# The second weight's sums on VectorE and later in the down stage; weight pieces one a step early in that stage

## The chip, the cores and the metric

One core of one Trainium2 chip. The metric is device microseconds of one launch. The six runs of the kernel before lie within 0.3% of one another (1125.70 to 1128.74 us), its eleven in the session of e17 and e18 within 0.7% (1124.67 to 1131.90 us), so an effect of 0.5% needs several runs of both kernels, interleaved. All runs told here were in the fast state and all gave correct results.

## The reference, cut to what matters

```python
# q, k, v: (8, 8, 576, 64) float32; w_ch1: (512, 2048); w_ch2: (2048, 512)
attn = softmax(q_c @ k_c.T / 8) @ v_c                 # in chunks of 64 rows
x = attn.transpose(0, 2, 1, 3).reshape(8, 576, 512)
u = x + real(fft(fft(x, axis=1), axis=2))             # Fourier mixing
un = (u - mean(u)) / sqrt(var(u) + 1e-6)
out = u + maximum(un @ w_ch1, 0) @ w_ch2
```

## The kernel before

Everything is fp32, and TensorE is meant never to stand still. The first batch's product with the first weight (up stage, steps t = 1 to 16) and with the second weight (down stage, L927, t = 17 to 32) run plainly. In the same steps the second batch's attention and Fourier products (L607), mixes (L659) and norm (L781, L782) are slipped in, and the weights, which arrive as 64-bit floats, are rounded to fp32 in 32 pieces (L295 to L306, on VectorE and ScalarE). From the second batch on, products are done in a form that needs sums of the weights' blocks. These sums are made once: `keep2` makes those of the second weight (16 sums in four groups), `keep1` those of the first. Each group is then written to DRAM by seven stores of 256 KB.

```python
    def keep2(i):
        ...
        to = xall[:, 2 * G:2 * G + 4, 0:DM] if i % 2 else yall
        ...
        for out_, in0, in1, op in (
            (o1, b12, b11, ALU.subtract), (o2, b22, o1, ALU.subtract),
            (o3, b22, b12, ALU.subtract), (o4, b21, o2, ALU.subtract),
        ):
            nc.gpsimd.tensor_tensor(out=out_, in0=in0, in1=in1, op=op)       # L854
            yield
        to = s2.rearrange("o p (m e) -> o p m e", m=HF)
        for o, a in enumerate((b11, o2, o1, o3, b21, b22, o4)):
            nc.sync.dma_start(out=to[o, :, m:m + 2], in_=a)                  # L858
        yield

    # in keep1(i), sums of the first weight, on GpSimd (L836), into yall or into rows of w2:
        for o, a in enumerate((a11, o2, o1, o3, a12, o4, a22)):
            nc.sync.dma_start(out=to[:, :, o, kk], in_=a...)                 # L840

    def operands(h1, m):        # first read of what keep1 has stored away
        nc.vector.tensor_tensor(out=xs[:, m], in0=h1[:, m, hi], in1=h1[:, HF + m, hi], op=ALU.add)   # L877
        ...
    # the loop over steps; round_next() rounds one piece
                if not heavy:
                    round_next()
                    if t <= 4 or t % 4 == 0 or t >= 18:
                        round_next()
                for _ in range(2):
                    if n_w > N_LAST + 2 and n_conv < 5 or n_w > len(pieces):
                        n_conv += 1
                        next(conv2, None)
```

`conv2` runs through `keep2` in small steps: a sum each, then the seven stores in one. Two properties matter below. SyncE issues nearly all loads and stores (145,296 of the 147,914 packets of before are in its queue q1), in program order. And VectorE works in program order too: L877 writes over memory from which `keep1` stores, so it waits until those stores are done (7.24 us in before), and everything of VectorE's behind it waits along.

Of the kernel before, what the change touches and what calls it, by code (L numbers as in the profile page):

```python
# [16 lines left out]
def kernel(  # L17
# [32 lines left out]
    nc = tc.nc  # L50
# [10 lines left out]
    KF = DFF // 128  # L61
# [79 lines left out]
    N_LATE, N_EARLY, N_LAST = 5, 8, 26  # L141
# [32 lines left out]
    def load(n):  # L174




        for src, dst, nm, eng in ((q, qs, "q", nc.sync), (k, ks, "k", nc.scalar if n == 0 else nc.sync)):
            if n < first[1]:  # L180
                i = 2 * n + (nm == "k")
                t = start[:, (4 + i) * DM:(5 + i) * DM].rearrange("p (j r d) -> p j (r d)", r=2, d=D)
            else:
                t = one_p.tile([128, NJ, 4 * D], FP32, tag=nm, name=nm)
            if n >= first[2]:
                (b0, c0), (b1, c1) = chunks(n)
                parts = [(0, 32, b0, min(c0, c1))] if b0 == b1 else [(0, 16, b0, c0), (16, 16, b1, c1)]
                for g in range(4):
                    e, x0 = g // 2, g % 2 * 32
                    for r0, rows, b, c in parts:  # L190
                        from_ = src[b, e:H:2, c * CH:c * CH + 4 * rows, :].rearrange("j (p t) d -> p j (t d)", t=4)
                        eng.dma_start(
                            out=t[32 * g + r0:32 * g + r0 + rows, :, 0:4 * D - 32],
                            in_=from_[:, :, x0:x0 + 4 * D - 32],
                        )
                dst[n] = t
                continue
            t = t.rearrange("p j (r d) -> p (j r) d", d=D)[:, 0:H]
            (b0, c0), (b1, c1) = chunks(n)
            if b0 == b1 and c1 == c0 + 1:  # L200
                parts = [(0, 128, b0, c0)]
            else:
                parts = [(0, CH, b0, c0), (CH, CH, b1, c1)]
            for p0, np_, b, c in parts:
                eng.dma_start(
                    out=t[p0:p0 + np_], in_=src[b, :, c * CH:c * CH + np_, :].rearrange("h p d -> p h d")
                )
            dst[n] = t
# [44 lines left out]
    def turn_dim_tables():  # L253
# [9 lines left out]
    pieces = [  # L263
        (w1[:, kk, f:f + 512], w_ch1[kk * 128:(kk + 1) * 128, f:f + 512])
        for f in range(0, DFF, 512)
        for kk in range(KD)
    ] + [(w2[:, m, :], w_ch2[m * 128:(m + 1) * 128, :]) for m in range(KF)]
# [8 lines left out]
    def load_weight(i):  # L276

        fit = [r for r in free if (i < N_EARLY or r < N_LATE) and (i < N_LAST or r > 1)]
        if i < len(pieces) and fit:
            raws[i] = fit[0]  # L280
            free.remove(fit[0])
            nc.sync.dma_start(out=raw(i).rearrange("p f r -> p (f r)"), in_=pieces[i][1].bitcast(U32))
# [560 lines left out]
    def keep2(i):  # L843

        m = 2 * i
        b11, b12 = w2[:, m:m + 2, 0:HM], w2[:, m:m + 2, HM:DM]
        b21, b22 = w2[:, HF + m:HF + m + 2, 0:HM], w2[:, HF + m:HF + m + 2, HM:DM]
        to = xall[:, 2 * G:2 * G + 4, 0:DM] if i % 2 else yall
        o1, o2, o3, o4 = (to[:, j].rearrange("p (m e) -> p m e", m=2) for j in range(4))
        for out_, in0, in1, op in (  # L850
            (o1, b12, b11, ALU.subtract), (o2, b22, o1, ALU.subtract),
            (o3, b22, b12, ALU.subtract), (o4, b21, o2, ALU.subtract),
        ):
            nc.gpsimd.tensor_tensor(out=out_, in0=in0, in1=in1, op=op)  # L854
            yield
        to = s2.rearrange("o p (m e) -> o p m e", m=HF)
        for o, a in enumerate((b11, o2, o1, o3, b21, b22, o4)):
            nc.sync.dma_start(out=to[o, :, m:m + 2], in_=a)  # L858
        yield
# [213 lines left out]
    with tc.manual_schedule():  # L1073
        nc.vector.memset(warm, 0.0)
        make_identity(nc, ident)
        nc.vector.memset(eps, 1e-6)
        nc.vector.memset(top[:, 0:1], float((896 + 255) << 20))
        nc.vector.memset(top[:, 1:2], float(255 << 23))
        nc.scalar.preload_act_table_set("natural_log_exp_and_others")
        first_rest = three_p.tile([128, XW], FP32, tag="y", name="first_rest")  # L1080
        for t in more_v + v_ring:
            nc.vector.memset(t[:, :, :, D:DV], 1.0)
        for n in range(first[1]):
            load(n)
            if n < 3:
                load_v(n)
        load_tables()
        load_weight(0)
        load_v(3)
        load_v(4)  # L1090
        load_dim_tables()
        for i in range(1, len(spaces)):
            load_weight(i)
        n_w = 0
        idle = ps_f.tile([128, 512], FP32, tag="ff", name="idle")
        early_xp = [ps_f.tile([128, 512], FP32, tag="ff", name="early_xp") for _ in range(2)], None

        def keep_warm(times):

            for _ in range(times):  # L1100
                nc.tensor.matmul(out=idle[:, 0:NQ], lhsT=warm[:, 0:128], rhs=warm[:, 0:NQ], start=True, stop=True)

        def round_next():
            nonlocal n_w
            if n_w <= len(pieces):
                round_weight(n_w)
                n_w += 1

        keep_warm(8)
        attention_early()  # L1110
        turn_dim_row()
        for step, _ in enumerate(fourier_early()):
            if step == 0:
                turn_dim_tables()
        round_next()
        PAUSE = 3

        def side(b):
            yield from attention(b)
            for _ in range(PAUSE):  # L1120
                yield
            yield from fourier(b)

        sides = [list_ for list_ in (side(b) for b in range(1, B))]
        sizes = []
        for b in range(1, B):
            n_tiles = first[b + 1] - first[b]
            sizes.append(4 * n_tiles + PAUSE + 2 + NM + b % 2 + (b == 1))
        done, cur = 0, 0
        begin = [0]  # L1130
        for g in range(NG):
            begin.append(begin[-1] + (KF if g < first_of[1] else 2 * HF) + (KF if g < first_of[2] else 2 * NO))
        ready_at = [begin[g] + (2 * KF - 7 if g < first_of[2] else 2 * HF + 4) for g in range(NG)]
        conv2 = iter([step for i in range(HF // 2) for step in [keep2(i)]])
        conv1 = iter([step for i in range(4) for step in [keep1(i)]])

        def chain(gens):
            for gen in gens:
                yield from gen

        n_conv = 0
        conv2, conv1 = chain(conv2), chain(conv1)
        t = 0
        for g in range(NG):
            for _ in mlp(g):
                t += 1
                heavy = False
                if cur < len(sides):
                    t0 = 2 if cur == 0 else ready_at[cur - 1]
                    t1 = ready_at[cur]  # L1150
                    due = min(sizes[cur], (t - t0) * sizes[cur] // (t1 - t0))
                    while done < due:
                        heavy = next(sides[cur], None) or heavy
                        done += 1
                    if t >= t1:
                        for _ in sides[cur]:
                            pass
                        cur, done = cur + 1, 0
                if not heavy:
                    round_next()  # L1160
                    if t <= 4 or t % 4 == 0 or t >= 18:
                        round_next()
                for _ in range(2):
                    if n_w > N_LAST + 2 and n_conv < 5 or n_w > len(pieces):
                        n_conv += 1
                        next(conv2, None)
                if t == begin[1] - 1:
                    for _ in conv2:
                        pass
                if begin[1] <= t < begin[1] + KF // 2:  # L1170
                    for _ in range(3):
                        next(conv1, None)
                if t == begin[1] + KF // 2:
                    for _ in range(NS2):
                        fetch(2)
                if t == begin[1] + KF:
                    for _ in range(NS1):
                        fetch(1)
# [49 lines left out]
```

## Time and profile before

| | before |
|---|---|
| time, median of the first 3 runs | 1126.54 us (1126.36 to 1127.37) |
| profiled span | 1124.9 us |
| TensorE busy | 1092.1 us (97%) |
| VectorE / ScalarE / GpSimd busy | 569.5 / 294.2 / 307.7 us |
| mean granted clock of TensorE | 0.996 |

TensorE is what bounds the kernel: only its 32.8 us of idle time and its stretches of half clock can be won. The prediction shows where it waits at 150 us. The part that it hardly shows, and that this study turned on, is SyncE's queue. Here are lines of its timeline; columns are the start of the issue in us, the time that issuing took (for several issues, from the first start to the last end, pauses included), the queue, the line of code, and destination <- source:

```profile
160.40 2.72 SPq L858 DMA_DIRECT2D s<-xall  x3
...
181.87 1.76 SPq L192 DMA_DIRECT2D q<-in_q_dram  x4
...
210.22 0.59 SPq L840 DMA_DIRECT2D s<-wa  x1
...
248.37 1.20 SPq L461 DMA_DIRECT2D first<-xall  x2
```

The first line belongs to the second group of `keep2`'s stores. It goes out before the next q and k loads (181.87). Groups three and four follow behind those loads, then `keep1`'s stores from 210.22 on, and at 248.37 the loads for the fold, from which the next Fourier products are made. VectorE's and TensorE's own timelines at the two places that depend on this queue (in brackets the idle time before, and what ended it):

```profile
245.30 0.42 DVE L877 TENSOR_TENSOR wb<-h 128x256 f32<-128x256 f32 x1 [7.24 <-DMA s<-wb]
```
```profile
267.10 1.73 PE L607 MATMUL z<-tk,pm 128*128 128x289 f32 x6 [0.34 <-POOL pm L496]
```

VectorE had stood 7.24 us for `keep1`'s stores, while TensorE waited only 0.34 us for the fold. GpSimd, which makes the fold, waits for SyncE's loads first, and then works with hardly a pause until TensorE can start:

```profile
252.55 1.28 POOL L480 TENSOR_TENSOR sum<-xall 128x512 f32<-128x512 f32 x1 [2.25 <-DMA xall<-first]
...
266.37 0.68 POOL L496 TENSOR_TENSOR pm<-two 128x256 f32<-128x256 f32 x1
```

### The profile page before, as it was taken

The numbers are of one execution on the slowest core, as the hardware profiler recorded it, in microseconds if no ns is written. First come the engines' busy times: TensorE is split into PE (matmuls) and PEld (weight loads), VectorE is DVE, ScalarE is ACT, GpSimd is POOL, SyncE is SP. The second block draws the span as 40 slices with busy tenths as digits, with TensorE's granted clock in tenths as the row PEclk, the third lists the DMA queues.
The fourth block names the chain that finished last, engine by engine and source line by source line (L and its number), as shares of the span: only waits on it lengthen the run. The fifth ranks groups of instructions, "written<-read, shape, count | busy, mean of one in ns | idle before, by whom it ended". The sixth has DMA issues, their size and how long they took to land. (4 is left out here: it accounts for less than half of the span.)

```text
span 1124.9 us, 18754 instructions
## 1 busy us (share of the span) xinstructions
PE 1092.1 (97%) x7036; PEld 846.0 (75%) x7036; DVE 569.5 (51%) x1194; ACT 294.2 (26%) x710; POOL 307.7 (27%) x436
## 2 busy tenths in 40 slices
PE   7999989999999999999999999899999999999998
PEld 5644445446887888778888888788888888888887
DVE  3899974332556355553545355645454434423521
ACT  4688443221112311222122211222132102201210
POOL 6400136325403340053105130154014400130130
PEclk9999989999999999999999999999999999999999
DMA  9767564688465636772567356763664346446332
GB/s 190 221 184 180 153 203 154 190 247 276 165 200 171 178 122 208 233 202 85 175 195 222 104 177 193 207 172 116 197 197 118 113 140 204 142 144 199 90 113 75
DMA packets 147914, 192.73 MB, mean 171 GB/s; under 512 B 66260, under 2 KB 104152, under 8 KB 140656
## 3 DMA queue, kind: packets, MB, share of 16 engines
q1 hardware_dynamic: 145296, 189.57, 56.1%
q0 software_dynamic: 928, 1.57, 0.6%
q8 instruction: 56, 0.92, 0.3%
q10 hardware_dynamic: 1600, 0.39, 0.2%
q14 instruction: 34, 0.28, 0.1%
HBM read 167.22 MB, written 24.12 MB: 170 GB/s over the span
## 5 line engine op out<-in xcount | busy, mean ns | idle before, releaser
L879 POOL TENSOR_TENSOR h<-h 128x256 f32<-128x256 f32 x64 | 55.3, 870 | 413.8 <-PE pb L973 303.3
L1020 PE MATMUL pa<-wb,h 128*128 128x256 f32 x512 | 116.1, 381 | 0.0
L1020 PE MATMUL pb<-wb,h 128*128 128x256 f32 x512 | 115.0, 381 | 0.0
L973 PE MATMUL pb<-unT,wa 128*128 128x256 f32 x448 | 106.6, 381 | 4.4 <-DVE wa L982 4.4
L973 PE MATMUL pb<-wa 128*128 128x256 f32 x448 | 107.3, 382 | 0.9 <-DMA wa<-s 0.9
L973 PE MATMUL pa<-unT,wa 128*128 128x256 f32 x448 | 107.8, 383 | 0.0
L1020 PEld LDWEIGHTS pa<-wb,h 128*128 128x128 f32 x512 | 95.8, 190 | 14.6 <-issue 1.6
L1020 PEld LDWEIGHTS pb<-wb,h 128*128 128x128 f32 x512 | 95.8, 190 | 12.9
L973 PEld LDWEIGHTS pb<-unT,wa 128*128 128x128 f32 x448 | 84.3, 190 | 18.5 <-DVE wa L982 7.0
L973 PEld LDWEIGHTS pb<-wa 128*128 128x128 f32 x448 | 83.4, 190 | 14.2 <-DVE wa L980 1.4
L973 PEld LDWEIGHTS pa<-unT,wa 128*128 128x128 f32 x448 | 83.2, 190 | 11.6
L988 ACT ACTIVATE h<-pa 128x256 f32<-128x256 f32 x56 | 21.5, 383 | 176.0 <-PE pa L973 142.8
L889 PE MATMUL up<-unT,wa 128*128 128x512 f32 x128 | 58.0, 599 | 2.4 <-ACT h L897 1.6
L980 DVE TENSOR_TENSOR wa<-pa,wa 128x256 f32<-128x256 f32 x56 | 23.8, 424 | 70.4 <-PE pa L973 70.3
L927 PE MATMUL dn<-wb,h 128*128 128x512 f32 x128 | 57.7, 599 | 1.3 <-ACT h L897 1.3
L1020 PE MATMUL pa<-wb,yall 128*128 128x256 f32 x256 | 58.2, 382 | 0.0
L973 PE MATMUL pa<-wa 128*128 128x256 f32 x224 | 54.0, 384 | 3.8 <-ACT wa L978 3.8
L906 PE MATMUL up<-unT,wa 128*128 128x512 f32 x128 | 57.5, 598 | 0.0
L1020 PE MATMUL pb<-wb,yall 128*128 128x256 f32 x256 | 57.1, 380 | 0.0
L1020 PE MATMUL pb<-wb 128*128 128x256 f32 x256 | 56.6, 379 | 0.0
L1020 PEld LDWEIGHTS pb<-wb 128*128 128x128 f32 x256 | 48.2, 190 | 6.3
L1020 PEld LDWEIGHTS pa<-wb,yall 128*128 128x128 f32 x256 | 47.7, 190 | 6.9 <-issue 0.5
(235 smaller groups left out, 1673.1 us busy)
## 6 DMA issues: line engine op xcount, KB each, us to landing
wb<-s SPq DMA_DIRECT2D x56, 1024.0 KB
wa<-s SPq DMA_DIRECT2D x196, 256.0 KB
xall<-in_moe_w_ch_dram SPq DMA_DIRECT2D x22, 512.0 KB
q<-in_q_dram SPq DMA_DIRECT2D x96, 112.0 KB
k<-in_k_dram SPq DMA_DIRECT2D x96, 112.0 KB
v<-in_v_dram SPq DMA_DIRECT2D x124, 64.0 KB
yall<-in_moe_w_ch_dram SPq DMA_DIRECT2D x10, 512.0 KB
s<-wb SPq DMA_DIRECT2D x20, 256.0 KB
```

Of the source, the lines that this page charges most:

```text
L879: nc.gpsimd.tensor_tensor(out=h1[:, m, hi], in0=h1[:, m, lo], in1=h1[:, m, hi], op=ALU.subtract)
L889: nc.tensor.matmul(out=up, lhsT=w1[:, kk, m * 128:(m + 1) * 128], rhs=unT[:, kk], start=(kk == 0), stop=(kk == KD - 1),)
L906: nc.tensor.matmul(out=up, lhsT=w1[:, kk, m * 128:(m + 1) * 128], rhs=unT[:, kk], start=(kk == 0), stop=(kk == KD - 1),)
L927: nc.tensor.matmul(out=dn, lhsT=h1[:, m, s * 128:(s + 1) * 128], rhs=w2[:, m, :], start=(m == 0), stop=(m == KF - 1),)
L973: nc.tensor.matmul(out=dst, lhsT=w[:, kk, r], rhs=rhs[o][:, kk], start=(o in (0, 2) and kk == 0), stop=(kk == 1), skip_group_check=True,)
L980: nc.vector.tensor_tensor(out=b, in0=dst, in1=a, op=ALU.add)
L988: nc.scalar.activation(out=h1[:, m, lo], in_=dst, func=ACTF.Relu)
L1020: nc.tensor.matmul(out=dst, lhsT=lhs[:, m], rhs=w[:, m], start=(o in (0, 2) and m == 0), stop=(m == HF - 1), skip_group_check=True,)
```

## The change

Its intent: the sums are cheaper on VectorE (0.69 us each) than on GpSimd (1.27 to 1.77 us) and no longer hold VectorE up from there; fewer weight pieces stand ahead of ScalarE's copy of the Fourier products, for which TensorE waits 5.2 us; and the sums, now VectorE's, are moved behind the norm of the second batch. (Not all of them are: in the trace of the changed kernel seven sums, at 168.04 to 170.65 and 180.04 to 182.05 us, still run ahead of the norm's first L781 at 181.97.)

```diff
-            nc.gpsimd.tensor_tensor(out=out_, in0=in0, in1=in1, op=op)
+            nc.vector.tensor_tensor(out=out_, in0=in0, in1=in1, op=op)
@@ the loop over steps
-                    if t <= 4 or t % 4 == 0 or t >= 18:
+                    if t <= 4 or t < KF and t % 4 == 0 or t >= KF + 7:
                         round_next()
-                for _ in range(2):
-                    if n_w > N_LAST + 2 and n_conv < 5 or n_w > len(pieces):
-                        n_conv += 1
-                        next(conv2, None)
+                if n_w > N_LAST + 2 and n_conv < 5:
+                    for _ in range(5 if t == KF + 8 else 0):
+                        n_conv += 1
+                        next(conv2, None)
+                elif n_w > len(pieces) and t >= KF + 10:
+                    for _ in range(3):
+                        next(conv2, None)
```

KF is 16. The sums' move takes their stores along: this is the part of the change that its description does not mention.

## The prediction

> **What bounds the kernel now.** I read the page first. Its busy line gives TensorE 1092.1 us of a span of 1124.9, so the whole kernel has 32.8 us of TensorE idle time, and only removing some of that, or raising a lowered clock, can shorten it. VectorE (569.5 us) and GpSimd (307.7 us) matter only where TensorE waits for them. Second, the waits of TensorE itself:
>
> ```profile
> PE z L607 <- ACT zr L635: 5.2, 1, 5.2
> PE pb L973 <- DVE wa L982: 4.4, 4, 1.3
> PE pa L973 <- ACT wa L978: 3.8, 7, 0.6
> PE pt L316 <- DVE un L784: 1.7, 6, 0.3
> ```
>
> Columns: total us, times, longest. One single wait of 5.2 us stands out, and it lies where the change works. Third, the order in time around it. L927 is the first batch's down product, L607 the two pairs of Fourier products of the second batch (a pair fills both buffers of its pool, so the second cannot start before ScalarE has emptied the first):
>
> ```profile
> 143.02 2.11 PE L607 MATMUL z<-tk,pm 128*128 128x289 f32 x8
> 145.06 0.76 PE L607 MATMUL z<-tk,pm_rest 64*128 64x289 f32 x4
> 145.75 3.70 PE L927 MATMUL dn<-wb,h 128*128 128x512 f32 x8
> 154.60 4.22 PE L607 MATMUL z<-tk,pm 128*128 128x289 f32 x8 [5.16 <-ACT zr L635]
> ...
> 160.41 3.70 PE L927 MATMUL dn<-wb,h 128*128 128x512 f32 x8
> ```
>
> The first pair is complete at 145.8, but ScalarE copies it only at 154.0. On ScalarE's own timeline:
>
> ```profile
> 152.65 0.71 ACT L298 ACTIVATE power<-power,top 128x512 uint32<-128x512 uint32 x1
> 153.39 0.72 ACT L299 ACTIVATE power<-power,top 128x512 uint32<-128x512 uint32 x1
> 154.01 0.35 ACT L632 COPY zf<-z 128x256 f32<-128x256 f32 x1
> ```
>
> L296 to L299 round weight pieces, two per step in program order before the copy; each waits for VectorE's chain of pieces, which runs late. Last, the windows (length, TensorE, weight loads, VectorE, ScalarE, GpSimd, then the granted clock):
>
> ```profile
> 149.40:154.60 5.20, 0.05 (x1) 0.00 (x0) 4.78 (x9) 4.35 (x10) 0.00 (x0) 0.82 0.73 209
> 154.60:158.80 4.20, 4.20 (x10) 2.56 (x10) 3.89 (x6) 2.36 (x6) 1.80 (x2) 0.50 1.07 397
> 158.80:160.40 1.60, 1.60 (x29) 0.79 (x28) 1.60 (x2) 0.00 (x0) 1.57 (x1) 0.76 0.53 188
> ```
>
> The wait also costs clock: at half clock from about 152.8 to 159.6, 5.0 us of it with work, so 2.5 us lost (the eight records of 2.11 us above take 4.22). The place costs 5.16 + 2.5 = 7.7 us.
>
> [...] the trace has 0.69 us for every such instruction on VectorE, against 1.27 for the same sums on GpSimd. [...] while GpSimd made these sums, one 0.69 us addition (L480) took 1.77 us and pieces at 140.3 lost 3 us.
>
> **The change part by part.** (1) The sixteen sums (L854) leave GpSimd, 16 x 1.27 = 20 us, and cost VectorE 16 x about 0.69 = 11 us. TensorE never waits for GpSimd here, so this saves nothing directly. (2) In the steps up to the Fourier products one piece per step is rounded instead of two. The instruction order shows four pieces (numbers 8 to 11) ahead of the first copy instead of seven; one goes between the two pairs, two behind the second, the last behind the rest tile's mix. (3) Four sums now stand on VectorE ahead of the first mix of the two main tiles, and three more ahead of the first scale-and-shift of the norm (L781).
>
> I replayed the queues with durations of this trace. Without GpSimd's sums VectorE gains 1.1 us at L480, and the pieces start at 133.5, 136.1 and 139.2 (a piece lands about 3.7 us after the buffer it reuses is released). ScalarE is through with the fourth at about 142, so the first pair is copied at 145.8 to 146.8. TensorE then starts the second pair at 149.45 at full clock: 2.11 + 0.6 + 0.6 = 3.3 us, to 152.8. The 7.7 us are gained at this point; the next down step needs weight row 7, done at 129.7.
>
> Now the path behind it. ScalarE empties the second pair (2.0 us, before: 160.55 to 162.57) until 154.9, then does the two pieces left for it, 2 x 1.95, until 158.8; the rest tile's mix, ready at 158.1, is copied by 159.2. VectorE: the rest tile's mix and statistics 2.54 (to 161.7), last piece and its close 2.6 + 2.0 (to 166.2), four sums 4 x 0.7 (to 169.0), first mix 3.67 (to 172.7), 0.92 until ScalarE has copied the next one (173.6), second mix 3.6 (to 177.2), softmax 1.35 (to 178.55), three sums 2.05 (to 180.6), L781 0.2. ScalarE then makes `un` in 0.8 (L782), so `un` stands at about 181.7. Before, it was this:
>
> ```profile
> 175.71 0.42 DVE L669 TENSOR_TENSOR y<-y,mix 128x255 f32<-128x255 f32 x1 [0.92 <-ACT y L665]
> ...
> 179.31 0.66 DVE L378 TENSOR_REDUCE mx<-sc 128x8 f32<-128x512 f32 x1
> 180.00 0.69 DVE L380 TENSOR_TENSOR ex<-sc,mx 128x512 f32<-128x512 f32 x1
> 180.61 0.20 DVE L781 TENSOR_SCALAR shift<-st,rstd 128x1 f32<-128x1 f32 x1
> ```
> ```profile
> 181.26 0.80 ACT L782 ACTIVATE un<-xall,shift,rstd 128x512 f32<-128x512 f32 x1
> ```
> ```profile
> 182.63 0.60 PE L316 MATMUL pt<-ident,un 128*128 128x128 f32 x4
> ```
>
> TensorE transposes that tile at 182.63, and `un` was ready at 182.1: only half a microsecond of slack. With 7.65 us gained, TensorE comes to this transpose at 175.0, but `un` comes at 181.7. It waits 6.7 us, and the gain left at this point is 182.63 - 181.7 = 0.9 us. [...] Sum: -0.9 + 2.5 = +1.6 us against before.
>
> Behind that I find slack: the three other tiles' `un` come at about 185, 190 and 194, TensorE wants them at about 188, 193 and 197. The DMA queue on SyncE is another matter. The second group of stores of these sums was issued at 160.4 and now comes behind the q and k loads, at about 185; this 4 us of issue time pushes a queue that from 182 to 254 waits only some 6 us in all. The first of the next stage's transfers stands at its end (248 to 256), and the wait of TensorE for the fold there is already 0.3 us. I allow 0 to 1.5 us, 0.3 in the middle. Predicted: 1126.5 + 1.6 + 0.3, rounded down for the chance that the new wait is shorter: 1127.8 us.
>
> **The rivals.** (a) The wait is simply gone: 1126.5 - 7.7 = 1118.9 us. For it: the only long wait of TensorE is the one that the change removes, and its cause (ScalarE behind two pieces a step) is right. Against it: the half microsecond of slack at 182.6, and about 4.9 us of sums put ahead of that point. (b) [...] if the chain is 3 us shorter than I reckon (pieces quicker, sums overlapped), TensorE waits 3.7 us, and the time is 1122.7 with the clock kept or 1125 without. (c) The DMA queue runs late and starves the second batch's up and down stage: 1129 to 1131. For it: the nearly gapless queue; against it: those 6 us of slack, and a later TensorE that asks later. (d) Missing weight rows in the down stage because of the slower rounding: rows 8 to 12 are done at 136 to 150, TensorE asks from 158 on; I give it nothing.
>
> **Range and chances.** The middle is my replay; its low side takes in rival (b), its high side (c); rival (a), at perhaps one in ten, falls outside: 1122.5 to 1130.5. Everything named lies within 0.7% of before, so within 2% gets 0.97; even all of the 7.7 us would be 0.7%. Faster 0.01, slower 0.02.
>
> **What would show it.** Right steps: the first pair copied about 146, the second at 149.5 with no wait and clock 1.0; a new wait of TensorE for `un` (L782) of 6 to 7 us before the transpose at about 181.7, with a clock of 0.5 behind it; VectorE without gaps from about 161 to 181, apart from a second at the second mix. Wrong: if the transpose starts near 175 there is no new wait and rival (a) holds; if it starts near 178 and the clock stays at 1.0, rival (b); if there is a new wait after 255 at the slabs or the fold, rival (c).

## The result, and the profile after

| | before | after |
|---|---|---|
| median of 6 runs each, same chip | 1126.69 us (1125.70 to 1128.74) | 1133.82 us (1131.61 to 1134.48) |
| ratio | | 1.0059 [1.0046, 1.0072] |
| profiled span | 1124.9 us | 1132.0 us |
| TensorE busy | 1092.1 us | 1092.5 us |
| mean granted clock | 0.996 | 0.994 |

A ratio is the mean time of one kernel's fast runs over that of the other's of the same rounds, so it is not quite the ratio of the medians. The kernel became 0.6% slower, about 6.6 us in the mean, and left the predicted range (1122.5 to 1130.5) on its high side.

TensorE's waits after the change (total us, times, longest):

```profile
PE pt L316 <- ACT un L782: 5.9, 1, 5.9
...
PE z L607 <- POOL pm L496: 2.4, 1, 2.4
PE xp L407 <- issue: 2.1, 1, 2.1
```

The wait of 5.2 us for the copy `zr` is gone from the list. One of 5.9 us for `un` has come, and two shorter ones that before had not, or hardly. TensorE's timeline shows where they are:

```profile
145.20 2.11 PE L607 MATMUL z<-tk,pm 128*128 128x289 f32 x8
...
151.46 2.11 PE L607 MATMUL z<-tk,pm 128*128 128x289 f32 x8
...
183.08 1.12 PE L316 MATMUL pt<-ident,un 128*128 128x128 f32 x4 [5.91 <-ACT un L782]
...
256.15 0.70 PE L407 MATMUL xp<-v,pT 64*64 64x65 f32 x32 [2.10 <-issue]
...
273.71 1.73 PE L607 MATMUL z<-tk,pm 128*128 128x289 f32 x6 [2.42 <-POOL pm L496]
```

The second pair of Fourier products (151.46) starts without a wait and takes 2.11 us where it took 4.22. The transpose at 183.08 waits 5.91 us and runs at half clock (four matmuls in 1.12 us where before had 0.60). ScalarE's timeline at the two places:

```profile
148.03 0.37 ACT L632 COPY zf<-z 128x256 f32<-128x256 f32 x1 [4.20 <-PE z L607]
...
182.21 0.81 ACT L782 ACTIVATE un<-xall,shift,rstd 128x512 f32<-128x512 f32 x1 [1.42 <-DVE shift L781]
```

ScalarE now waits for TensorE at the first copy instead of the other way round, and the norm's `un` waits for VectorE's L781. The windows show the clock (length, TensorE, weight loads, VectorE, ScalarE, GpSimd, granted clock, DMA share, GB/s):

```profile
180.00:184.00 4.00, 0.92 (x5) 0.92 (x6) 3.96 (x8) 1.44 (x2) 0.20 (x1) 0.51 0.00 0
184.00:190.00 6.00, 6.00 (x26) 3.29 (x28) 3.28 (x8) 1.93 (x4) 0.00 (x0) 0.76 0.88 263
```

VectorE is busy 3.96 of 4 us ahead of the transpose, and the clock is at half from 180.1 for 6.83 us. SyncE's queue after the change:

```profile
169.48 1.30 SPq L858 DMA_DIRECT2D s<-yall  x3
...
183.22 1.76 SPq L192 DMA_DIRECT2D q<-in_q_dram  x4
...
187.40 1.74 SPq L858 DMA_DIRECT2D s<-xall  x3
...
215.52 0.59 SPq L840 DMA_DIRECT2D s<-wa  x1
...
254.97 1.21 SPq L461 DMA_DIRECT2D first<-xall  x2
```

Only the first group of stores (169.48) still goes out ahead of the q and k loads. The second (187.40) stands behind them, so 21 stores follow the loads instead of 14. `keep1`'s first store is 5.3 us later than before (210.22) and the fold's loads 6.6 us (248.37). VectorE's L877 follows:

```profile
251.48 0.42 DVE L877 TENSOR_TENSOR wb<-h 128x256 f32<-128x256 f32 x1 [11.06 <-ACT pT L393]
```

It is 6.2 us later. (The profile names ScalarE's copy as what ended this wait. For the same wait it names the stores in the kernel before, and in two later kernels, e13 and e11, where it is 13.0 and 12.6 us long; so I take it for the stores here too.) VectorE does the next scaling of the attention behind it, at 255.36, and TensorE's product at 256.15 waits for the room which that makes.

TensorE does the same 7036 matmuls in the same order in both kernels, so the difference of the starts of the same matmul tells where time went. I call it lateness: after minus before, in us, at places named by the time in the trace of before.

| trace | 143 | 160 | 182.5 | 200 | 254 | 270 | end |
|---|---|---|---|---|---|---|---|
| after | 2.2 | -5.6 | 0.5 | 2.4 | 4.5 | 6.6 | 6.7 |

The 2.2 us at 143 were there from the first loads on (by 30 us). From there to 160 TensorE gained 7.8, lost all of it and 0.2 more by 200, and lost another 4.2 in the two new waits between 200 and 270. Behind 270 nothing changed.

### The profile page after: what moved, and what is told of

Same layout as the page of the kernel before. It is cut to its first block, busy times and chain, and to the rows that moved or that the text cites. A ratio compares the mean times of both kernels' runs of the same rounds, so it can differ in the third digit from the quotient of the medians.

```text
span 1132.0 us, 18751 instructions
## 1 busy us (share of the span) xinstructions
PE 1092.5 (97%) x7036; PEld 847.4 (75%) x7036; DVE 572.2 (51%) x1210; ACT 293.7 (26%) x710; POOL 286.7 (25%) x420
## 3 DMA queue, kind: packets, MB, share of 16 engines
q0 software_dynamic: 928, 1.57, 0.6%
## 5 line engine op out<-in xcount | busy, mean ns | idle before, releaser
L988 ACT ACTIVATE h<-pa 128x256 f32<-128x256 f32 x56 | 21.5, 384 | 176.0 <-PE pa L973 143.0
L676 POOL TENSOR_TENSOR xall<-y,xall 128x513 f32<-128x513 f32 x14 | 21.3, 1520 | 131.4 <-DVE y L670 131.4
```

The lines of the kernel that those rows point to most:

```text
L676: eng.tensor_tensor(out=x[:, 0:w], in0=y[:, 0:w], in1=x[:, 0:w], op=ALU.add)
L988: nc.scalar.activation(out=h1[:, m, lo], in_=dst, func=ACTF.Relu)
```

## The experiments

Two theories of the loss at the start: it is jitter of the first loads, or the changed program begins slower. Three of the loss behind 200 us: the order of SyncE's queue, the transfers on the DMA engines, or TensorE's own new wait at 183. In all, 18 kernels ran; none was refused.

### e1, e2: both kernels again

No edit.

> Control. The profiled run of the changed kernel is 2.2 us late already at the second batch's Fourier products (145.2 against 143.0), behind an instruction order that is the same up to there; it waited 3.3 us for the first load of k where the kernel before waited 1.8. Theory J: this start is jitter of the first loads, and belongs to no kernel. Then this unchanged kernel shows times of 1125.5 to 1129, and its profile may start those products anywhere from 143 to 145.5. Rival S: the start is a property of the build; then this one shows 143.0 again, within 0.5.

> Control for the changed kernel: 1131 to 1134.5. J: the Fourier products start anywhere from 143 to 145.5; S: at 145.2 again, within 0.5. Both: a wait of 5.5 to 7 us before the first transpose of the norm with half clock behind it, and two waits of about 2 us each after 245 (the score-value product and the second batch of Fourier products) that come from the late queue of stores and loads.

e1: 1127.39 us, ratio 0.9998 [0.9983, 1.0014]. e2: 1134.18 us, 1.0059 [1.0043, 1.0074]. The ratio repeats to the digit. The start does not: e1 was 1.0 us late at 143 and e2 1.1 us early (earlier even than theory J had allowed), so this is jitter from run to run. e2 was 0.4 us early at 200 us and 4.4 us late at 270: again 4.8 us lost in that stretch (waits of 1.50 and 1.90 us, and a stretch of half clock of 3.41 us behind the second). It also lost 4 us at about 605 us, where TensorE waited 2.7 us for a weight slab and fell to half clock; the first profile of the same kernel shows nothing there.

### e3, e4: one part of the change alone

e3 has only the new rounding, e4 only the engine of the sums:

```diff
# e3, on before
-                    if t <= 4 or t % 4 == 0 or t >= 18:
+                    if t <= 4 or t < KF and t % 4 == 0 or t >= KF + 7:
# e4, on before
-            nc.gpsimd.tensor_tensor(out=out_, in0=in0, in1=in1, op=op)
+            nc.vector.tensor_tensor(out=out_, in0=in0, in1=in1, op=op)
```

> Only the rounding of the pieces is slowed; sums stay on GpSimd, two steps of them per step. Theory P (the seven sums ahead of the norm make the new wait): the 5.2 us wait for the first pair of Fourier products is gone with its clock loss, the transpose of the norm waits 0 to 2.5 us and the clock stays at 1.0. Theory Q (the SyncE queue is a second bound right behind): with the queue where it was and TensorE 6 us ahead, the waits after 245 grow to 3 to 6 us, and the time is 1121 to 1126. Rival to Q (the waits after 245 belong to the changed kernel's order alone): 1119.5 to 1121.

> Only the sums move to VectorE, placed as before; the SyncE queue keeps its order. [...] the wait for the first pair shrinks from 5.2 to about 2.5 us[...]. Four sums stand ahead of the norm's first shift: its transpose waits 1 to 3 us. Q: the queue of stores is no later than before against the clock of the wall, so waits after 245 are 1 to 4 us because TensorE is earlier; time 1121.5 to 1126. Rival[...]: the wait stays at 5 us or grows, 1126 to 1130.

e3: 1126.70 us, 0.9996 [0.9979, 1.0012]. e4: 1124.69 us, 0.9971 [0.9956, 0.9986]. e3 missed its ranges (1121 to 1126 at most). It was 8.2 us early at 160, but `un` was waited for by 2.9 us, longer than expected, with half clock for 3.41 us, so 3.5 us were left at 200; at 270 it was level with before, these 3.5 us lost as well. e4 lay in its range; the wait for the first pair fell from 5.16 to 1.89 us (the 2.5 us expected were an estimate), with half clock for 3.41 us behind it, and e4 gained only 2.7 us up to 200 but kept 1.9. It leaves the second group of stores ahead of the loads, as before. So neither the rounding nor VectorE's sums make the kernel slower by themselves; something at a nearly fixed time behind 200 us takes what was won.

### e5: the sums' stores from GpSimd's queue

```diff
# on after, in keep2
-            nc.sync.dma_start(out=to[o, :, m:m + 2], in_=a)
+            nc.gpsimd.dma_start(out=to[o, :, m:m + 2], in_=a)
```

> The changed kernel with the 28 stores of the second weight's sums issued from GpSimd's queue instead of SyncE's; all else as in the changed kernel. Theory Q (the SyncE queue, put late by stores that moved behind the q and k loads, costs about 2 us before the last score-value product of the second batch and about 2 us at the next Fourier products): both waits after 245 fall below 0.5 us, the wait of 5.9 us for the norm and its half clock stay, and the time is 1126.5 to 1129.5. Rival R (those waits come from the sums' load on VectorE or from the late start of the sums themselves): the waits stay, 1131 to 1134.5.

1130.27 us, 1.0014 [0.9998, 1.0031]. The stretch from 200 to 270 cost 0.3 us in place of 4.2: the late waits go with the stores (none at L407, 0.7 us at L607). The time lies above the expected range (1126.5 to 1129.5): GpSimd, which issues them, came to its own part of the norm later, and the wait for `un` grew to 7.3 us, with half clock for 10.24 us. That the one caused the other is likely but not tested.

### e6, e7, e8: all sums later

```diff
# e6, on after: the block for conv2 becomes
+                if n_w > len(pieces) and t >= KF + 11:
+                    for _ in range(5):
+                        next(conv2, None)
# e7: e6 with e5's edit
# e8: e7, and no pieces rounded in one step
-                if not heavy:
+                if not heavy and t != KF + 8:
```

> The changed kernel with all sixteen sums placed behind the norm's first shift (five steps of them in each of the last four steps before the second batch's up stage); stores on SyncE. Theory P (the seven sums ahead of the norm made the new wait): the transpose of the norm waits under 2.5 us and the clock stays at 1.0, so about 6 us are gained by the 190th us. Theory Q: now all four groups of stores stand behind the q and k loads, one group more than in the changed kernel, 4 to 5 us of issue; the waits after 245 grow from 4 to 8 to 12 us in sum and eat it all: 1128 to 1135. Rival (no Q): 1119 to 1122.

> Both cures together: sums behind the norm's first shift, their stores from GpSimd's queue. P and Q together: no wait over 2.5 us at the norm, none over 0.7 after 245; 1119.5 to 1122.5. If GpSimd's queue is slow in issuing (28 stores ahead of its sums for the first weight), the first weight's stores come late and a wait shows after 245 or at the first slab: 1122 to 1127.

> As the one before, and the last two weight pieces rounded one step later, behind the mixes of the two main tiles, which takes another 4.6 us out of the chain to the norm: its transpose waits under 0.3 us. 1118 to 1121.5, 1 to 2 us less than the one before; the same as that one if the norm was no longer waited for there.

e6: 1133.79 us, 1.0051 [1.0037, 1.0066]. e7: 1129.63 us, 1.0013 [0.9998, 1.0028]. e8: 1130.14 us, 1.0025 [1.0010, 1.0040]. e6 is the telling one: the wait for `un` fell from 5.9 to 1.9 us, TensorE was 2.5 us early at 200 instead of 2.4 late, and the kernel was no faster, since at 254 it was 7.4 us late behind a wait of 6.2 us at L407. All 28 stores stood behind the loads:

```profile
257.26 1.15 PE L407 MATMUL xp<-v,pT 64*64 64x65 f32 x32 [6.25 <-issue]
```

e7 missed both of its ranges (1119.5 to 1127). It shows that GpSimd's queue is no way out when all stores come late: the wait of 6.2 us at L407 was there again, and the q, k and v loads took 4.15, 5.47 and 4.72 us to issue instead of 2.34, 1.80 and 2.65. e8 missed its range (1118 to 1121.5) too, and was a slip of mine: the two pieces I moved still stand ahead of L781, so it does not test a shorter norm chain.

### e9, e10, e12: the first weight's stores from GpSimd's queue

```diff
# e9 on after, e10 on e4, e12 on e11: in keep1
-            nc.sync.dma_start(out=to[:, :, o, kk], in_=...)
+            nc.gpsimd.dma_start(out=to[:, :, o, kk], in_=...)
```

> The changed kernel with the first weight's 28 stores (not the second's) issued from GpSimd, right behind the sums that make them; on SyncE they stand behind loads and the batch's output stores. Theory Q2 (what is late after 245 is this last group of stores, kept back by the in-order SyncE queue and by transfers that bunch up behind 185; VectorE's operand sums wait for them, and the score-value product waits for VectorE): the stores run ahead in the gap from 200 to 216, both late waits fall below 0.6 us, the norm's wait and half clock stay: 1126.5 to 1129. Rival R (the loads themselves are late): the late waits stay above 1.5 us, 1131 to 1134.5.

> The version with the sums alone moved to VectorE (1124.7), with the first weight's stores from GpSimd. Q2: the 0.7 us that it lost between 254 and 267 come back, 1123 to 1124.7; its gain of 2.7 us at the 200th us is all there is. Rival R: 1124.5 to 1126.

> As e11, with the first weight's stores from GpSimd. P and Q2 together: the gain of 6.5 to 7.7 us is kept to the end, 1119 to 1121.5. If transfers themselves are the limit from 185 to 250, 1122 to 1126.

e9: 1139.79 us, 1.0117 [1.0089, 1.0146]. e10: 1131.05 us, 1.0037 [1.0018, 1.0056]. e12: 1134.43 us, 1.0076 [1.0043, 1.0108]. All three are slower than the kernels they were made from, and outside every range that I had given. VectorE's timeline in e9:

```profile
238.63 1.08 DVE L333 STREAM_TRANSPOSE qT<-q 128x512 f32<-128x512 f32 x1 [15.35 <-DMA q<-in_q_dram]
```

With the stores out of its way SyncE still was slow: four q loads took 6.36 us from the first to the last, nearly all of it issuing, and four k loads 8.64, of which 2.45 were issuing and the rest pauses (before 2.47 and 1.81). VectorE's work on q started 14 us later than before, and TensorE waited 9.4 us at L365, the scores of the attention. A theory of the queue's order alone falls with this. Here SyncE's own loads were held up with the stores issued elsewhere. (GpSimd's queue in before, q0 with 928 packets, is of another kind, software_dynamic; e15 below shows a delay with ScalarE's stores too, whose queue q10 is of SyncE's kind, hardware_dynamic.)

### e11: the lead without the sums ahead of the norm

```diff
# on after
-                if not heavy:
+                if not heavy and not KF + 8 <= t < KF + 11:
...
-                if n_w > N_LAST + 2 and n_conv < 5: ...
+                if t == KF + 6 or n_w > len(pieces) and t >= KF + 12:
+                    for _ in range(5):
+                        next(conv2, None)
```

> Slow rounding, sums on VectorE: the first group of sums in the step of the first Fourier pair, where VectorE sits idle waiting for ScalarE, the last two pieces behind the norm's first shift, the other sums behind those; all stores on SyncE. P (seven sums and the piece behind which they stand held the norm up): the norm's transpose waits under 0.5 us, clock 1.0 all through, 6.5 to 7.7 us gained by the 200th us (start jitter apart). Q2: one group of stores more stands behind the q and k loads than before the change, so 4 to 6 us of it are lost again by the 270th us: 1123 to 1127. Rival (no Q2): 1119 to 1121.

1126.78 us, 0.9999 [0.9980, 1.0019]. The first transpose of `un` did not wait at all: TensorE was 7.6 us early at 182.5 and 6.2 us at 200, as the change had meant it. At 254 it was 0.3 us early. TensorE's timeline:

```profile
249.12 1.15 PE L407 MATMUL xp<-v,pT 64*64 64x65 f32 x32 [3.60 <-issue]
```

So the norm chain was not what lost the 6 us at the end; the 21 stores behind the loads were suspected, and the next four runs gave the seven that are new among them to the kernel before as a dose.

### e13 to e16: seven stores more, in the kernel before

Seven stores of already rounded rows go to a scratch place that nobody reads. In e13 they stand on SyncE behind the third group, e14 has them of one partition (2 KB each), e15 issues them from ScalarE, and e16 puts them behind the second group, at 165 us. (In these kernels the lines are shifted: L408 is L407, L859 is L858, L881 is L877; L862 is the added store.)

```diff
# e13, in keep2 behind the seven stores
+        if i == 2:
+            for o in range(NO):
+                nc.sync.dma_start(out=s3[o], in_=w2[:, m:m + 2, 0:HM])
# e14: in_=w2[0:1, m:m + 2, 0:HM]     e15: nc.scalar     e16: if i == 1
```

> The kernel before with seven more stores of 256 KB (second weight's rows into a scratch place nobody reads), issued on SyncE right behind the third group of stores, so behind the q and k loads at about 186 to 192 us. That is the amount of stores that the change pushed behind these loads, without anything else of the change. Theory Q (the order of the SyncE queue) and theory X (transfers compete for the DMA engines) both expect what the changed kernel showed behind 200 us: TensorE late by 2 to 5 us at 270 us against the kernel before, new waits at the chunks' products (L407) or the Fourier products (L607), 1128.5 to 1132 us. If it costs under 1 us, the late stores are not the cause and both fall.

> The same seven more stores on SyncE at the same place, but of one partition, 2 KB each instead of 256 KB: issue time, nearly no transfer. Theory Q: as the full stores, 2 to 5 us late at 270 us, if a small store takes as long to issue. Theory X: under 0.7 us late, 1126 to 1127.7 us.

> The same seven full stores of 256 KB at the same place in the program, but issued on ScalarE, so that nothing is added to SyncE's queue: transfer, no issue time there. Theory Q: under 0.7 us late at 270 us, 1126 to 1127.7 us. Theory X: as e13, 2 to 5 us late, with q and k and the first weight's stores landing later although SyncE issues them at the same place in its order.

> The seven full stores on SyncE, but behind the second group, at about 165 us, where the DMA engines stand still until 182 us. Both theories: they are done by about 171 us, under 0.7 us late at 270 us, 1126 to 1127.7 us. If this costs 2 us or more, it is not the place behind the q and k loads that counts, and both theories fall.

| | median, us | ratio | lateness at 200 | at 254 | at 270 |
|---|---|---|---|---|---|
| e13: 256 KB each, SyncE | 1132.66 | 1.0044 [1.0028, 1.0061] | 0.9 | 6.6 | 6.9 |
| e14: 2 KB each, SyncE | 1132.20 | 1.0041 [1.0020, 1.0061] | -0.6 | 2.9 | 3.9 |
| e15: 256 KB each, ScalarE | 1131.78 | 1.0040 [1.0025, 1.0055] | 0.0 | 1.7 | 4.9 |
| e16: as e13, at 165 us | 1126.77 | 1.0001 [0.9986, 1.0017] | -1.3 | -1.3 | -0.2 |

The dose alone costs at least as much as the change's late loss (in e13 a little more than the 2 to 5 us at 270, and the 1132 us, that I had expected), and the same dose at 165 us costs nothing (1.0001; in before the DMA share is 1.04 from 164 to 166 us, 0.03 from 168 to 170 and 0.00 from 170 to 182). SyncE's timeline of e13:

```profile
191.35 5.41 SPq L862 DMA_DIRECT2D s<-wb  x7
```

And that of e14:

```profile
190.35 4.31 SPq L862 DMA_DIRECT2D s<-wb  x7
```

A store of 2 KB occupies the queue for 4.31/7 = 0.62 us, one of 256 KB for 0.77 (the first of the seven apart, 0.54 to 0.60 and 0.62 to 0.64 us each): most of that time is the issue, not the bytes. TensorE's new wait in e13 has the form of that after the change:

```profile
256.60 1.08 PE L408 MATMUL xp<-v,pT 64*64 64x65 f32 x32 [3.97 <-issue]
```

The theory of transfers alone expected e14 under 0.7 us, and falls. e15 is not a clean opposite, and my expectation that nothing would be added to SyncE was wrong. The issues came earlier than meant, at 180.4 to 185.5, and met the loads:

```profile
181.44 3.70 SPq L193 DMA_DIRECT2D q<-in_q_dram  x4
```

The q loads took 3.70 us instead of 1.76; 1.7 us of it is a pause ahead of the fourth, which the profile puts down to q loads that had not landed. ScalarE itself stood 3.93 us behind its own issues. So SyncE's queue is the path, and in these runs it was lengthened in two ways: by an issue in it (e14: 0.62 us each), and with stores from elsewhere, beside which its own issues took longer (e7: 1.2 to 1.5 us for one k load instead of 0.4) or stood still (e15: 1.7 us; e9: 6.2 us of 8.64). What part each has in e13 stays open.

### e17, e18: the reverse

Three of a group's seven stores store rounded rows as they are and need no sum. e17 is e11 with seven such stores issued from 151 to 160 us (in the trace of after the DMA share is 0.02 from 156 to 158 us and 0.00 from 158 to 160); e18 is e4 with six of them at about 155 us. (L859 is L858, L873 the early stores, L891 is L877.)

```diff
# e17; e18: groups 2 and 3, when the last piece is rounded
+                if t == KF + 8:
+                    keep2_raw(1, (0, 4, 5))       # stores of b11, b21, b22
+                    keep2_raw(2, (0, 4, 5))
+                    keep2_raw(3, (0,))
```

> e11 (its seven to eight us of lead at 182 us were all lost again by 267 us) with seven of its stores, those that store rounded rows as they are and need no sum, issued at about 158 us, when the DMA engines stand still, instead of behind the q and k loads. 14 stores stay behind the loads, as many as in the kernel before, and the queue reaches them about seven us sooner. If the stores behind the loads are what took e11's lead, the first weight's stores, the fold loads and with them TensorE come 4 to 6 us earlier from 245 us on: late by -3 to -6 us at 270 us against the kernel before, 1120.5 to 1124 us. If something else stands at an absolute time there, TensorE is within 1 us of the kernel before at 270 us, 1126 to 1127.5 us.

> e4 (sums on VectorE, the old rounding and placing; 2.7 us of lead at 182 us, 1124.7 us) with the six stores of plain rows of the third and fourth groups issued at about 155 us instead of behind the q and k loads: 8 stores stay there instead of 14. TensorE's lead at 182 us stays the 2.7 us of e4, since nothing of VectorE's or ScalarE's order changes, and the loss of 0.7 us between 254 and 267 us should go: 1123 to 1124.5 us. Against e17 it shows whether lead or stores limit: if the stores alone were worth 4 us even without lead, it would be 1121 us or less.

e17: 1124.20 us (1122.26 to 1125.34), 0.9967 [0.9947, 0.9986]. e18: 1122.67 us (1120.61 to 1125.60), 0.9958 [0.9936, 0.9980], the fastest kernel of the study. e17 went through the place at 254 with its 6.0 us of lead unspent: the wait at L407 was gone. It then met the next one:

```profile
262.98 3.23 PE L607 MATMUL z<-tk,pm 128*128 128x289 f32 x6 [2.25 <-POOL pm L496]
```

2.25 us of wait and 1.6 us lost to half clock left 2.5 us at 270, a little less than I had expected (3 to 6; 1124.0 us at most). The fold's loads were at 243.88 there, 4.5 us earlier than before, not 6. e18 had the 3.6 us of lead at 200 and 4.2 at 270, with no wait in between. L877 waited for the stores only shortly:

```profile
238.08 0.43 DVE L891 TENSOR_TENSOR wb<-h 128x256 f32<-128x256 f32 x1 [3.59 <-DMA s<-wb]
```

That start is 7.2 us earlier than in the kernel before. e18 came out just below the range that I expected (1123 to 1124.5), and in its trace the wait of 1.85 us for the Fourier products did not cost clock as e4's of 1.89 did, which has nothing to do with the stores. The stores' share, by one trace each, is the difference between a loss of 0.7 us (e4) and a gain of 0.6 between 200 and 270. The timed runs do not show it: the intervals of e4 and e18 overlap widely. For e17 they do: it gains 0.3% over e11, just clear of noise, though the two were timed in different sessions, each against the kernel before.

### The ledger

Lateness against the first trace of before, in us, with the number of `keep2`'s stores that SyncE issues behind the q and k loads, the start of the fold's loads in its queue, the start of the Fourier products made from the fold (267.10 us in before), and TensorE's wait just ahead of those.

| trace | late at 200 | stores behind | fold's loads | products | apart | wait | late at 270 | end |
|---|---|---|---|---|---|---|---|---|
| before | 0 | 14 | 248.37 | 267.10 | 18.7 | 0.34 | 0 | 0 |
| e1 before again | 0.6 | 14 | 249.00 | 267.75 | 18.8 | 0.42 | 0.7 | 0.2 |
| after | 2.4 | 21 | 254.97 | 273.71 | 18.7 | 2.42 | 6.6 | 6.7 |
| e2 after again | -0.4 | 21 | 251.27 | 269.85 | 18.6 | 1.90 | 4.4 | 7.4 |
| e3 rounding only | -3.5 | 14 | 246.93 | 265.45 | 18.5 | 1.91 | -0.1 | -0.2 |
| e4 VectorE only | -2.7 | 14 | 246.44 | 265.17 | 18.7 | 1.09 | -1.9 | -2.4 |
| e6 all sums later | -2.5 | 28 | 255.78 | 274.51 | 18.7 | 0.34 | 7.4 | 8.0 |
| e11 replaced | -6.2 | 21 | 247.78 | 267.06 | 19.3 | none | -0.2 | 0.1 |
| e13 dose | 0.9 | 14 + 7 | 255.56 | 274.04 | 18.5 | 0.68 | 6.9 | 6.6 |
| e16 dose early | -1.3 | 14 | 247.87 | 266.89 | 19.0 | 1.48 | -0.2 | -0.2 |
| e17 e11, rows early | -6.0 | 14 | 243.88 | 262.98 | 19.1 | 2.25 | -2.5 | -2.1 |
| e18 e4, rows early | -3.6 | 8 | 241.53 | 263.04 | 21.5 | none | -4.2 | -4.7 |

Wherever TensorE waits there, the products start 18.4 to 19.1 us behind the fold's loads (the table leaves out e5, e7, e14 and e15, where it is 18.4 to 18.9; in e8, e9, e10 and e12 it is 19.5 to 29.6 without a wait, since TensorE had stood 4.4 us at L407 or 6.3 to 11.3 us at L365 before). These 18 to 19 us are the loads and GpSimd's work on the fold, so a faster fold, which no run tried, should shorten them. The time that SyncE reaches these loads thus sets the earliest time for TensorE, whatever its lead; in e6 and e13 it had lost most of its time already at L407, for `keep1`'s stores of the same queue. The time of the loads follows from two things: how early the queue starts, which moves with the lead, and how many stores it has to issue. e3 shows a third: with 14 stores its loads came only 1.4 us earlier with a lead of 3.5, and the stretch of half clock behind the wait took the rest. Its queue started 3.5 us earlier but paused 2.3 us longer in all. So it was in e11 (2.6 us more of pauses) and in e17 (5.3): in these three runs the queue that started earlier waited more for other work, and the early start was kept only in part. One trace can differ from the mean of the timed runs by some 3 us (e5's trace ended 4.8 us late, its timed mean is 1.6 us up), so the ledger tells where, and the ratios how much. One source of this shows: half clock at the wait of 5 us at about 150 us lasted 6.83 us in before, e1, e13 and e14, but 3.41 us in e15 and e16, which are the same up to there; that is 1.7 us.

## Why the prediction was wrong

The first half held. The first pair was copied at 148.0, within 0.1 us of its products (predicted: at once, with the run's own start 2.2 us late); the second pair did not wait and ran at full clock; the gain up to 160 was 7.8 us in this trace and in the repetition (predicted 7.7). The new wait for `un` came, 5.9 us long (predicted 6.7), and VectorE was busy ahead of it with no pause longer than the one predicted (0.92 us at the second mix). 1.7 us of the gain were left at 182.5 in both traces (predicted 0.9). That the clock would be halved behind this wait was an estimate, from the 5.16 us wait of before, which was followed by 5.0 us of work at half clock. Half clock lasted 3.8 us behind the restart in the first trace and 4.9 in the second and cost 1.9 and 2.5 us (the prediction's sum has 2.5, as much as before lost). From 143 to 200 the sum was +0.2 us in the first trace and +0.7 in the second, where the prediction had +1.6: within 1.4 us, on the good side.

The step that failed is the queue: "this 4 us of issue time pushes a queue that from 182 to 254 waits only some 6 us in all", for which it allowed "0 to 1.5 us, 0.3 in the middle". That term measured 4.2 us in the first trace, 4.8 in the second, and 5.0 us in the mean of timed runs when given alone as a dose (e13). The mechanism had been named, as rival (c), and the profile shows the signs that rival was to have: waits behind 255 us at the fold. Two things in it were wrong. The pauses in the queue were taken for slack, but they did not shrink: `keep1`'s first store came 5.3 us later, the q loads behind its pause 5.3 us later too (218.51 became 223.81), and the fold 6.6. Counted from the records between the q loads of 181.87 and the fold's loads, SyncE's 92 issues take 57.9 of 66.5 us before; in the changed kernel 99 issues take 63.5 of 71.7 us. That is 5.6 us of issuing more and 0.3 us of pauses less (8.2 us instead of 8.6). Most of the pauses are the short gaps between one issue and the next; only one is longer than 0.4 us (1.57 us ahead of 217.14, later 1.21), and the profile puts it down to output stores of the same queue. And the wait of 0.34 us at the fold was read as "already 0.3 us" rather than as "no slack at all"; that VectorE's L877 passes the delay on to the attention at L407 was not seen.

The rest of the miss is not a step of the working. In the first trace 2.2 us were jitter of the start, in the second 4 us were a wait for a slab at 605 us. The timed runs lost 6.6 us in the mean; the queue and the norm account for 4.4 to 5.5 of it (4.2 + 0.2; 4.8 + 0.7). Whether the remaining one to two microseconds are chance or a systematic part of the later stages stays open.

What would have told it beforehand was in the profile of before: between the q loads of 181.87 and the fold's loads SyncE's track is filled with issues for 57.9 of 66.5 us. e14 agrees that issuing counts there: its seven stores of 2 KB, 0.62 us each in the queue, cost the kernel 4.6 us in the mean.

## What to carry to other kernels

When work is moved to a later place, look at what it drags along: here the sums, 0.69 us each, could be placed so that they cost nothing (e11: no wait at the first transpose), but the seven stores behind them could not follow them for free, since they crossed from a stretch of 12 us in which the DMA engines stood still (share 0.00 from 170 to 182 us) into one in which the queue had no room. The pauses in SyncE's queue were not slack here: with 5.6 us more of issues they fell only from 8.6 to 8.2 us, and the one pause of over 0.4 us was put down to output stores of the same queue. And a gain on the path counts only up to the next time that is fixed by something else: e11 won 7.6 us and kept none, until e17 took seven stores out of the way.

## What the traces show of issuing and of the clock

- Issuing: seven stores of 2 KB took 4.31 us to issue (e14), seven of 256 KB 5.41 us (e13), and the small ones alone made the kernel 1.0041 times as long.
- SyncE's loads with stores issued on other engines: four q loads went out within 6.36 us instead of 2.47, four k loads within 8.64 us instead of 1.81 (e9), and four q loads within 3.70 us instead of 1.76, with a pause of 1.7 us in it (e15). The runs do not separate the causes.
- The clock: half clock for 3.41 us followed single waits of TensorE of 1.89 us (e4), 1.90 us (e2) and 2.25 us (e17), while a wait of 1.85 us at the place of e4's kept the clock in e18, and so did the changed kernel's waits of 2.10 and 2.42 us. The length of the wait alone does not tell these cases apart, and what does is not shown here. A wait of about 2 us thus cost some 1.7 us more in clock, half of 3.41, or nothing.
